# First gate of an attention and two-expert-layer kernel: no emptying of the queue at pair 12, PE pieces behind the products with the values, token rows in a queue of their own

## The chip, the cores and the metric

One Trainium2 chip, one core of it. The metric is the device time of one execution in microseconds (us). PE is TensorE, DVE is VectorE, ACT is ScalarE, POOL is GpSimd, SP is SyncE, which issues most DMAs.

## The reference

Three stages follow one another; each reads what the last one made.

```
attn  q, k, v: B=4, H=8, S=576, D=64
      s = q k^T / 8;  keep s >= max(s) - tau;  softmax over the kept;  x = attn v       -> x: 2304 tokens x 512
moe1  logits = x w_gate + log1p(exp(x w_noise)) * noise;  two best of 8 experts
      weights = softmax of these two;  out = sum of weight * (relu(x w1[e]) w2[e])       w1: 512x1024
moe2  tokens with x w_skip > 0 go to their one best expert and get weight * its output added
```

## The kernel before

*Attention.* The work is 16 pairs (a batch and two heads, laid on 128 partitions), and each pair has nine units: the 576 query rows of the two heads come as four full tiles of 128 for each head and one mixed tile. A unit makes scores S on PE (line 291), the row maximum on DVE (299), the exponential on ACT (301), the mask and sum on DVE (330), then the transposes T of the masked scores on PE (`emit_T`, 340), which ACT copies out as pt (342, 344). A pair has two chunks, and each ends in products with the values (`av`, 390 and 393, tile x) and a normalization by DVE (400, tile xT). Before that the row sums are inverted (355), POOL spreads them as rb (357, and 359 and 360 for the second chunk), and PE transposes them along with a left-over part of the scores (`extra`, 368 and 369; `extra_mixed`, 375 and 376).

A loop over the 144 units, `for u in range(NU)`, writes the instructions out in the order in which the engines take them: no scheduler moves them. In one round stand S of unit u+2, maximum and exponential of u+1, T of u-1, then products of chunks due at that time (table `AV`), then the mask of u. Counted from the start of a pair, units 2, 3, 4, 6, 7 and 8 hold products with the values; 0, 1 and 5 hold none.

*The first gate.* As soon as all tokens of some tiles are there, the gate of the first expert layer runs for them beside the next pairs: for 4 tiles after pair 3, for 5 after pair 7, for 4 after pair 11 (`GATES`); the last 5 tiles follow after attention. `gate1` is a generator: PE pieces (logits lg, their transpose, the ranks rk at lines 135 and 136), some 45 small DVE steps, and then scatters on POOL that write a token's number and weight to its expert's list in DRAM (`scatter`: a memset at 168, a DMA at 169; two for each tile). Between two scatters it waits `apart` steps. `rows1` (409) transposes a tile of tokens into rows and stores them. A generator yields 2 when its next thing is a PE piece, and 1 when this step is to end; `step(q, 1, False)` doesn't run a generator that stands before a PE piece. The gate and its rows lie in the queue `bg`, which is stepped three times in a round, the third time with PE pieces allowed.

All of these pieces, T's output and the pieces that follow write to one PSUM bank through `bank(...)`, so that each must be emptied before the next may write.

*Early experts.* At pair 12 the memory of the tokens of batches 0 and 1 is given back (`early_pool`), and the first two experts e0a and e1a prepare in it: `place_early` counts their tokens (ct, line 630; cntE, 632, then 711, 713, 715 on DVE), `load_early` loads their lists (meta, 559), `load_ids` makes the indices tid and gid (568, 570) and gathers the tokens (177), `early_xt` transposes them (xt, 584) and splits them in two (594 on ACT, 595 on DVE). `early_raw` loads weights (549, 551). After attention the weights are split (w1h, 821 on ACT; w1l, 822 on DVE or POOL) and the experts' products h (612) begin.

Of the kernel before, what the change touches and what calls it, by code (L numbers as in the profile page):

```python
# [39 lines left out]
def attention_moe_moe(ctx, tc, qT, kT, vm, vr, tau, wgn, noise, w1a, w2a, wsg, w1b, w2b, out):  # L40
# [143 lines left out]
    asked = {}  # L184

    lag = [4]
    apart = [4]

    def settle():
        for _ in range(lag[0]):  # L190
# [2 lines left out]
    def step(q, n=1, pe=True):  # L193

        while q and n > 0 and (pe or asked.get(id(q[0])) != 2):
            try:
                r = asked[id(q[0])] = next(q[0])
                n = 0 if r else n - 1
            except StopIteration:
                asked.pop(id(q.pop(0)), None)  # L200


    def pool(stack, name, bufs, side="left", **kw):
        return stack.enter_context(tc.tile_pool(name=name, bufs=bufs, side=side, reuse_waits="tile", **kw))
# [21 lines left out]
    def bank(nm):  # L226
        return banks[0](nm)
# [5 lines left out]
    def xcols(t):  # L233
        return lambda kd: xTs[t * 128 // HN][:, kd, t * 128 % HN:t * 128 % HN + 128]
# [171 lines left out]
    def rows1(t):  # L406
        ps = bank("tr")
        for kd in range(KD):
            nc.tensor.transpose(ps[:, kd * 128:(kd + 1) * 128], xcols(t)(kd), ident)
        xr = xr_p.tile([128, DM], F32, name="xr")  # L410
        nc.scalar.activation(xr, ps, AF.Copy)
        nc.sync.dma_start(x1[t * 128:(t + 1) * 128, :], xr)
# [119 lines left out]
    def expert(n, w1, w2, row0, kind, share=None):  # L532
        x = Ex()
        x.n, x.w1, x.w2, x.row0, x.kind, x.share = n, w1, w2, row0, kind, share
        x.raw, x.s1, x.s2 = (share.raw, share.s1, share.s2) if share else ({}, {}, {})
        x.native = n == 1
        x.places = share.places if share else {}
        x.ahead = x.fine = x.keep = False
        x.load = None
        x.rows = N  # L540
        x.home = None
        x.hid, x.sums, x.hh = {}, {}, None
        return x
# [9 lines left out]
    e0a, e1a = (expert(EARLY1[e], w1a, w2a, e * 128, 1) for e in range(2))  # L553
    e0a.rows, e1a.rows = 9 * 128, 13 * 128

    def load_meta(x, slots, row, small, idx=None, bufs=2):
        x.meta = small.tile([128, CAP1, 2], F32, name="meta", bufs=bufs)[:, :x.n]
        if idx is None:
            nc.sync.dma_start(x.meta, slots[row:row + x.n * 128, :].rearrange("(i p) c -> p i c", p=128))
        for i in range(0 if idx is None else x.n):  # L560
            gather(x.meta[:, i], slots, idx[:, i:i + 1])
        x.gid = small.tile([128, CAP1], I32, name="gid", bufs=bufs)[:, :x.n]
        x.tid = small.tile([128, CAP1], I32, name="tid", bufs=bufs)[:, :x.n]
# [3 lines left out]
    def load_ids(x, apart=[]):  # L567
        nc.vector.tensor_copy(x.tid, x.meta[:, :, 0])
        if x.kind == 1:
            nc.vector.tensor_scalar(x.gid, x.meta[:, :, 0], float(x.rows - 1), None, op0=OP.min)  # L570
            for i in range(x.n):
                gather(x.xs[:, i], x1, x.gid[:, i:i + 1], x.rows)
            return
        nc.gpsimd.memset(spacer, 0.0)
        for i in range(x.n):
            g = gather(x.xs[:, i], x2, x.tid[:, i:i + 1], bounds_check=N - 1, oob_is_err=False)
            for p in puts + apart:
                tc.declare_no_dep(g.ins, p.ins, reason="rows of other tokens")
            gets.append(g)

    def xt(x, i):
        ps = bank("xt")
        for kd in range(KD):
            nc.tensor.transpose(ps[:, kd * 128:(kd + 1) * 128], x.xs[:, i, kd * 128:(kd + 1) * 128], ident)
        ps = ps.rearrange("p (k c) -> p k c", k=KD)
        if x.native:
            x.xf = xp[0].tile([128, KD, 128], F32, name="xf")
            nc.scalar.activation(x.xf, ps, AF.Copy)
            return
        if i == 0:  # L590
            p, w = (x.home, x.n * 128) if x.home else (xp[0], SL1)
            x.xh, x.xl = rows2 if x.kind == 2 else (p.tile([128, KD, w], F32R, name=nm) for nm in ("xh", "xl"))
        o = x.xh[:, :, i * 128:(i + 1) * 128]
        nc.scalar.activation(o, ps, AF.Copy)  # L594
        nc.vector.tensor_tensor(x.xl[:, :, i * 128:(i + 1) * 128], ps, o.bitcast(F32), op=OP.subtract)  # L595
# [41 lines left out]
    bg = []  # L637
    fq = [fills()]
    pq, bq = [], []
# [6 lines left out]
    def at(u, phase, f, *a):  # L646
        plan.setdefault((u, phase), []).append((f, a))
# [7 lines left out]
            bg.append(f())  # L655
        return put

    WAITS = ((7, 10), (6, 0))
    GATES = {(3, 1): (0, 4), (7, 1): (4, 5), (11, 1): (9, 4)}

    def gate_and_rows(t0, n):
        rows = list(range(t0, t0 + n))
        for k, tok in enumerate(gate1(t0, n)):
            yield tok
            if k > 6 and k % 3 == 0 and rows:
                yield 2
                rows1(rows.pop(0))
                yield 1

    ectx = ExitStack()  # L670
    early = {}

    def early_pool():
        while bg:
            step(bg)
        xctx.close()
        p = early["p"] = pool(ectx, "early", 1)
        for x in (e0a, e1a):
            x.home = p
        early["h"] = [p.tile([128, AHEAD, EARLY1[0] * 128], F32R, name=nm) for nm in ("hhE", "hlE")]  # L680
# [6 lines left out]
    def load_early(x, e):  # L687
        x.xs = early["p"].tile([128, max(EARLY1), DM], F32, name="xs")
        load_meta(x, slots1, e * N, early["p"])

    def early_rows(x, e):
        yield from place_early(e)
        load_early(x, e)
        for _ in range(WAITS[e][0]):
            yield 1
        load_ids(x)
        for _ in range(WAITS[e][1]):
            yield 1

    def early_xt():  # L700
        for i in range(e0a.n):
            yield 2
            xt(e0a, i)
            yield 1

    def place_early(e):

        yield 2
        c = counts(run1, f"E{e}")
        yield  # L710
        nc.vector.tensor_scalar(c, c, -1.0, float(EARLY1[e] * 128), op0=OP.mult, op1=OP.add)
        yield
        nc.vector.tensor_scalar(c, c, 0.0, first_lane, op0=OP.max, op1=OP.mult)
        yield
        nc.vector.tensor_add(run1[:, e:e + 1], run1[:, e:e + 1], c[:, e:e + 1])
        yield
# [23 lines left out]
    for u in range(NU):  # L740
        g, c, t, hh = UNITS[u]
        if (c, t, hh) == (0, 0, 0):
            if g + 1 < len(PAIRS):
                load_v(g + 1)
            if g == 12:
                early_pool()
                fq.append(early_raw())
                bq.extend((early_rows(e0a, 0), early_xt()))
            if g == len(PAIRS) - 1:
                pq.append(early_split())  # L750
        if (c, t, hh) == (0, 0, 0) and g + 2 < len(PAIRS):
            load_qk(g + 2)
        if (c, t, hh) == (1, 3, 0) and g + 2 < len(PAIRS):
            pq.append(prep(g + 2))
        if u + 2 < NU:
            emit_S(u + 2)
        else:
            early_mm1(u + 2 - NU)
        if u + 1 < NU:
            emit_max(u + 1)  # L760
        step(bg, 1, False)
        run(u, "mid")
        if u % 2 == 0:
            emit_th(u)
        step(bg, 1, False)
        step(bq)
        if u:
            emit_T(u - 1)
        run(u, "pe")
        run(u, "end")  # L770
        emit_stt(u)
        step(pq)
        step(bg)
        if u % 4 == 3:
            step(fq)
        if (t, hh) == ((1, 1) if c == 0 else (4, 0)):
            k = (g, c)
            sums1(*k)
            at(u + 1, "mid", sums2, *k)
            at(u + 2, "pe", extra, *k)  # L780
            if c:
                at(u + 2, "pe", extra_mixed, g)
            for kt, (d, ph) in enumerate(AV[c]):
                at(u + d, ph, av, *k, kt)
            at(u + NORM[c][0], NORM[c][1], norm, *k)
            if k in GATES:
                at(u + 7, "end", bg.append, gate_and_rows(*GATES[k]))
                if k[0] == 11:
                    at(u + 7, "end", bg.append, early_rows(e1a, 1))
        if (c, t, hh) == (1, 2, 1):  # L790
            while pq:
                step(pq)
# [308 lines left out]
    for f in range(AHEAD, KF):  # L1101
# [4 lines left out]
          rows=[])  # L1106
# [340 lines left out]
    for k, x in enumerate(seq):  # L1447
        nx = seq[k + 1] if k + 1 < len(seq) else None
        rows = [r for r in seq[k + 1:k + 2] if k and not r.native] + [r for r in seq[k + 2:k + 3] if r.native]
# [56 lines left out]
```

## Time and profile before

| | |
|---|---|
| median of 3 runs | 1064.68 us (1064.45 to 1065.57) |
| the profiled execution | 1069.96 us, its span 1068.2 us |
| mean granted clock of PE | 0.977 of full speed |
| busy in the span | PE 994.7 us (93%), DVE 583.4, ACT 494.5, POOL 306.0 |
| first-gate scatters and rows | beside pairs 4 to 15 of attention |

Rows of the trace say when an instruction started (us from the span's start), how long it took, engine, line, operation, out<-in, and in brackets the engine's idle time before it and what ended it. Sixteen DMA engines serve the core; a matmul's end is modelled, so idle times of PE are good to about a tenth of a us.

### The profile page before, as it was taken

The numbers are of one execution on the slowest core, as the hardware profiler recorded it, in microseconds if no ns is written. First come the engines' busy times: TensorE is split into PE (matmuls) and PEld (weight loads), VectorE is DVE, ScalarE is ACT, GpSimd is POOL, SyncE is SP. The second block draws the span as 40 slices with busy tenths as digits, with TensorE's granted clock in tenths as the row PEclk, the third lists the DMA queues.
The fourth block names the chain that finished last, engine by engine and source line by source line (L and its number), as shares of the span: only waits on it lengthen the run. The fifth ranks groups of instructions, "written<-read, shape, count | busy, mean of one in ns | idle before, by whom it ended". The sixth has DMA issues, their size and how long they took to land. (4 is left out here: it accounts for less than half of the span.)

```text
span 1068.2 us, 16937 instructions
## 1 busy us (share of the span) xinstructions
PE 994.7 (93%) x6262; PEld 781.5 (73%) x6262; DVE 583.4 (55%) x1480; ACT 494.5 (46%) x941; POOL 306.0 (29%) x417
## 2 busy tenths in 40 slices
PE   6999999997989898999999999999999986899995
PEld 3555555554545796889889898989887775798894
DVE  6887888796776561553323342433323365577453
ACT  4766766664656441443333333333333232555352
POOL 3121143126204543221312222221322456222210
PEclk9999999998999899999999999999999998799998
DMA  6334354235320563453534445252453730766550
GB/s 151 102 87 128 109 163 88 71 93 128 122 67 1 182 194 79 130 177 90 148 77 138 111 128 120 77 158 68 109 168 78 267 115 18 283 207 197 183 220 16
DMA packets 54856, 134.76 MB, mean 126 GB/s; under 512 B 20043, under 2 KB 26475, under 8 KB 46064
## 3 DMA queue, kind: packets, MB, share of 16 engines
q1 hardware_dynamic: 41344, 107.17, 31.9%
q0 software_dynamic: 13424, 26.45, 10.8%
q8 instruction: 51, 0.84, 0.3%
q14 instruction: 37, 0.30, 0.1%
HBM read 112.64 MB, written 23.69 MB: 128 GB/s over the span
## 5 line engine op out<-in xcount | busy, mean ns | idle before, releaser
L626 DVE SCALAR_TENSOR_TENSOR hl<-h,hh 128x128 fp32r<-128x128 f32 (+3 forms) x157 | 80.1, 510 | 177.8 <-ACT hh L625 160.8
L853 PE MATMUL y<-w2h,hh 128*128 128x512 f32 x418 | 170.5, 408 | 1.2 <-ACT w2h L821 1.2
L625 ACT ACTIVATE hh<-h 128x128 fp32r<-128x128 f32 (+3 forms) x157 | 71.4, 455 | 202.2 <-PE h L612 153.3
L853 PE MATMUL y<-w2h,hl 128*128 128x512 f32 x418 | 164.3, 393 | 0.0
L853 PE MATMUL y<-w2l,hh 128*128 128x512 f32 x418 | 163.5, 391 | 0.2 <-DVE w2l L822 0.2
L612 PE MATMUL h<-xh,w1h 128*128 128x320 f32 (+2 forms) x596 | 154.7, 312 | 3.3 <-ACT xh L594 1.4
L612 PE MATMUL h<-xh,w1l 128*128 128x320 f32 (+2 forms) x596 | 152.3, 308 | 3.2 <-POOL w1l L822 3.2
L612 PE MATMUL h<-xl,w1h 128*128 128x320 f32 (+2 forms) x596 | 153.0, 309 | 1.6 <-DVE xl L595 1.6
L299 DVE TENSOR_REDUCE nm<-s 128x1 f32<-128x576 f32 x144 | 108.7, 755 | 49.9 <-PE s L291 48.9
L291 PE MATMUL s<-kr,qr 64*128 64x288 f32 (+1 forms) x640 | 112.9, 461 | 8.3 <-DVE kr L274 5.4
L301 ACT ACTIVATE e<-s,nm 128x576 f32<-128x576 f32 x144 | 106.3, 738 | 15.8 <-DVE nm L299 14.0
L342 ACT ACTIVATE pt<-tp 128x512 f32<-128x512 f32 x128 | 76.5, 597 | 74.1 <-PE tp L340 65.6
L612 PEld LDWEIGHTS h<-xh,w1h 128*128 128x128 f32 x596 | 105.9, 192 | 5.5 <-ACT xh L594 1.9
L612 PEld LDWEIGHTS h<-xh,w1l 128*128 128x128 f32 x596 | 106.1, 192 | 3.4 <-POOL w1l L822 3.4
L612 PEld LDWEIGHTS h<-xl,w1h 128*128 128x128 f32 x596 | 106.2, 192 | 2.8 <-DVE xl L595 2.7
L330 DVE SCALAR_TENSOR_TENSOR P<-s,th,e 128x576 f32<-128x576 f32 x128 | 103.4, 808 | 4.4 <-DVE foa L109 0.3
L862 POOL DMA_INDIRECT out_dram<-yo,tid x35 | 55.6, 1588 | 169.7 <-ACT yo L861 92.7
L340 PEld LDWEIGHTS tp<-ident,P 128*128 128x128 f32 x512 | 54.5, 142 | 57.1 <-issue 14.3
L853 PEld LDWEIGHTS y<-w2h,hl 128*128 128x128 f32 x418 | 78.7, 188 | 17.6
L853 PEld LDWEIGHTS y<-w2h,hh 128*128 128x128 f32 x418 | 79.0, 189 | 16.2 <-ACT w2h L821 1.7
L340 PE MATMUL tp<-ident,P 128*128 128x128 f32 x512 | 85.2, 290 | 5.1 <-DVE xl L595 2.9
L853 PEld LDWEIGHTS y<-w2l,hh 128*128 128x128 f32 x418 | 79.1, 189 | 14.5 <-DVE w2l L822 0.5
(270 smaller groups left out, 1457.4 us busy)
## 6 DMA issues: line engine op xcount, KB each, us to landing
rw<-in_w1a_dram SPq DMA_DIRECT2D x18, 1024.0 KB
rw<-in_w2a_dram SPq DMA_DIRECT2D x18, 1024.0 KB
qr<-in_qT_dram SPq DMA_DIRECT2D x30, 288.0 KB
rw<-in_w1b_dram SPq DMA_DIRECT2D x8, 1024.0 KB
rw<-in_w2b_dram SPq DMA_DIRECT2D x8, 1024.0 KB
kr<-in_kT_dram SPq DMA_DIRECT2D x96, 72.0 KB
out_dram<-zx SPq DMA_DIRECT2D x9, 512.0 KB
x<-xr SPq DMA_DIRECT2D x18, 256.0 KB
```

The costliest lines, as they stand in the source:

```text
L291: nc.tensor.matmul(s[o, i, 0:SH], qr[r, h, t * 128:min((t + 1) * 128, S)], kr[r, h if t < 4 else 2 * h], start=True, stop=True)
L299: nc.vector.tensor_reduce(nm, s, axis=AX.XY, op=OP.max, negate=True)
L301: nc.scalar.activation(e, s, AF.Exp, bias=nm)
L330: nc.vector.scalar_tensor_tensor(o.rearrange("p (a b) -> p a b", a=2), s, th, e, op0=OP.is_ge, op1=OP.mult, accum_out=a)
L340: nc.tensor.transpose(ps[:, kt], P[:, c0 + kt * 128:c0 + (kt + 1) * 128], ident)
L342: nc.scalar.activation(ch["pt"][:, :, hh, (t % 2) * 128:(t % 2 + 1) * 128], ps, AF.Copy)
L612: nc.tensor.matmul(ps[:, c, 0:m], w[:, kd, :], v[:, kd, a:a + m], start=(kd == 0 and j == 0), stop=(kd == KD - 1 and j == 2))
L625: nc.scalar.activation(dh, src, AF.Relu)
L626: nc.vector.scalar_tensor_tensor(dl, src, 0.0, dh.bitcast(F32), op0=OP.max, op1=OP.subtract)
L853: nc.tensor.matmul(y, h[:, i * 128:(i + 1) * 128], w, start=(f == 0 and j == 0), stop=(f == KF - 1 and j == 2))
L862: nc.gpsimd.indirect_dma_start(out=x2[:, :], out_offset=bass.IndirectOffsetOnAxis(ap=tid, axis=0), in_=yo, in_offset=None, compute_op=OP.a ...
```

## The change

`apart` is 2 instead of 4. Where the memory is given back at pair 12, only the rows that still wait are written out, and the gate's generator stays in its queue; the early experts' first steps (`early_rows`) go into the same queue, behind the gate. The rows of the three gates go to a queue `rq`. PE pieces are taken by `spare_pe`, which runs after the products in units 2, 3, 4, 6, 7 and 8 only: first the gate if it stands before a PE piece, else one tile of rows, else the other queues. The queue `bq` may no longer start a PE piece ahead of T. `early_ids` is split off from `early_rows` and, for the first expert, put into `bq`; `early_xt` waits until tid is there and 8 steps more. For the second expert, `early_rows` comes behind the gate of pair 11 as before.

```diff
-    apart = [4]
+    apart = [2]
...
-    WAITS = ((7, 10), (6, 0))
+    WAITS = (4, 6)
...
-    def gate_and_rows(t0, n):
+    rq = []
+
+    def gate_and_rows(t0, n, beside=False):
         rows = list(range(t0, t0 + n))
+        if beside:
+            rq.extend(rows)
+            yield from gate1(t0, n)
+            while rq:
+                yield 2
+                if rq:
+                    rows1(rq.pop(0))
+            return
...
+    def spare_pe():
+
+        if bg and asked.get(id(bg[0])) == 2:
+            step(bg)
+        elif rq:
+            rows1(rq.pop(0))
+        else:
+            step(bq)
+            step(bg)
...
     def early_pool():
-        while bg:
-            step(bg)
+        while rq:
+            rows1(rq.pop(0))
...
     def early_rows(x, e):
+        while not early:
+            yield 1
         yield from place_early(e)
+        if e == 0:
+            bq.insert(0, early_ids(x, e))
+        else:
+            yield from early_ids(x, e)
+
+    def early_ids(x, e):
         load_early(x, e)
-        for _ in range(WAITS[e][0]):
+        for _ in range(WAITS[e]):
             yield 1
         load_ids(x)
-        for _ in range(WAITS[e][1]):
-            yield 1
 
     def early_xt():
+        while not hasattr(e0a, "tid"):
+            yield 1
+        for _ in range(8):
+            yield 1
...
-                bq.extend((early_rows(e0a, 0), early_xt()))
+                bq.append(early_xt())
...
-        step(bq)
+        step(bq, 1, False)
         if u:
             emit_T(u - 1)
         run(u, "pe")
         run(u, "end")
         emit_stt(u)
         step(pq)
-        step(bg)
+        if u % 9 in (2, 3, 4, 6, 7, 8):
+            spare_pe()
+        else:
+            step(bg, 1, False)
...
-                at(u + 7, "end", bg.append, gate_and_rows(*GATES[k]))
-                if k[0] == 11:
-                    at(u + 7, "end", bg.append, early_rows(e1a, 1))
+                at(u + 7, "end", bg.append, gate_and_rows(*GATES[k], True))
+                if k[0] > 3:
+                    at(u + 7, "end", bg.append, early_rows(*((e0a, 0) if k[0] == 7 else (e1a, 1))))
```

The order of POOL at the start of pair 12, before: the last of the scatters of batch 1's gate (slots is the experts' list), and behind them the copies of the row sums, rb.

```order
L168 MEMSET spacer 1x1
L169 DMA slots_60<-mt_2864,ii_2887 18432x2
L168 MEMSET spacer 1x1
L169 DMA slots_60<-mt_2878,ii_2917 18432x2
L357 COPY rb<-sm 128x256
L359 COPY rb<-sm 128x128
L360 COPY Pm<-Pm 128x64
L357 COPY rb<-sm 128x256
L274 TENSOR_SCALAR kr<-kr,qsc 128x288 x3
```

And POOL at the same copies in the changed kernel:

```order
L274 TENSOR_SCALAR kr<-kr,qsc 128x288
L168 MEMSET spacer 1x1
L169 DMA slots_60<-mt_2878,ii_2917 18432x2
L357 COPY rb<-sm 128x256
L359 COPY rb<-sm 128x128
L360 COPY Pm<-Pm 128x64
L168 MEMSET spacer 1x1
L169 DMA slots_60<-mt_2864,ii_2887 18432x2
L168 MEMSET spacer 1x1
L169 DMA slots_60<-mt_2878,ii_2917 18432x2
```

The copies rb of pair 11's second chunk stood behind a block of eight scatters; now one scatter stands right ahead of them, behind a scaling of kr, and six scatters follow them ahead of the next rb.

The order of PE in pairs 13 and 14, with the two xt pieces of the first expert (584), as the difference of the two kernels:

```order
 L390 MATMUL x<-pt,v 64x320 x4
+L584 MATMUL xt<-ident,xs 128x128 x4
 L291 MATMUL s<-kr,qr 128x288 x2
 L340 MATMUL tp<-ident,P 128x128 x4
 L390 MATMUL x<-pt,v 64x320 x4
+L584 MATMUL xt<-ident,xs 128x128 x4
 L291 MATMUL s<-kr,qr 128x288 x2
 L340 MATMUL tp<-ident,P 128x128 x4
 L393 MATMUL x<-rr,vz_174 128x320
 L291 MATMUL s<-kr,qr 128x288 x2
-L584 MATMUL xt<-ident,xs 128x128 x4
 L340 MATMUL tp<-ident,P 128x128 x4
```

An xt piece stood between S and T and now stands between products with the values and S. The piece of the counts, ct, moves in the same way in pair 12, from between S and T of its second round to behind products of its seventh.

The order of PE at the end of attention, with the counts for the second expert, as the difference:

```order
 L375 MATMUL em<-ident,Pm 128x128
 L376 MATMUL em<-ident,rb 128x128
-L390 MATMUL x<-pt,v 64x320 x8
+L390 MATMUL x<-pt,v 64x320 x4
+L630 MATMUL ct<-run_113,ones 128x8
+L390 MATMUL x<-pt,v 64x320 x4
 L393 MATMUL x<-rr,vz_174 128x320
-L630 MATMUL ct<-run_113,ones 128x8
 L157 MATMUL lg<-xT_172,wgn_t 32x128 x16
```

The counts move from behind the last products to between them.

## Rows read from the trace of the kernel before

**Rows 1.** The page, busy time and share of the span by engine.

```profile
PE 994.7 (93%) x6262; PEld 781.5 (73%) x6262; DVE 583.4 (55%) x1480; ACT 494.5 (46%) x941; POOL 306.0 (29%) x417
```

**Rows 2.** Windows by pair: length, busy us by engine (instructions), PEclk, DMA share, GB/s.

```profile
81.44:100.04 18.60, 18.26 (x123) 9.95 (x123) 15.28 (x37) 12.75 (x22) 4.16 (x7) 1.00 0.43 127
100.04:122.35 22.31, 21.56 (x168) 12.09 (x168) 16.59 (x49) 14.53 (x28) 4.15 (x7) 1.00 0.28 89
122.35:142.33 19.98, 19.38 (x130) 10.70 (x130) 17.66 (x61) 13.88 (x25) 4.17 (x7) 1.00 0.65 198
179.75:203.47 23.72, 22.18 (x173) 12.67 (x173) 15.95 (x40) 14.86 (x29) 4.16 (x7) 1.00 0.21 61
203.47:225.29 21.82, 20.78 (x140) 11.60 (x141) 17.98 (x58) 14.56 (x26) 4.16 (x7) 1.00 0.45 122
244.33:270.48 26.15, 20.59 (x124) 11.15 (x123) 15.96 (x45) 12.80 (x22) 13.62 (x25) 0.87 0.51 135
...
292.79:317.33 24.54, 20.97 (x140) 11.64 (x142) 18.95 (x64) 15.06 (x27) 1.21 (x4) 1.00 0.24 76
```

**Rows 3.** Timeline, first half of pair 12: start, us, engine, line [idle before <-releaser].

```profile
245.61 1.02 POOL L169 DMA_INDIRECT slots<-mt,ii  x1 [0.17 <-issue]
...
246.88 0.58 SPq L549 DMA_DIRECT2D rw<-in_w1a_dram  x1
...
247.06 0.18 DVE L355 RECIPROCAL sm<-sm 128x5 f32<-128x5 f32 x1
...
249.32 0.39 PE L630 MATMUL ct<-run,ones 128*128 128x8 f32 x2
...
251.59 0.17 DVE L632 COPY cntE<-ct 128x8 f32<-128x8 f32 x1 [2.32 <-remote]
...
251.81 0.66 PE L340 MATMUL tp<-ident,P 128*128 128x128 f32 x4 [2.10 <-DVE cntE L632]
...
254.41 0.60 ACT L342 ACTIVATE pt<-tp 128x512 f32<-128x512 f32 x1 [4.51 <-remote]
254.58 0.97 POOL L169 DMA_INDIRECT slots<-mt,ii  x1 [0.23 <-issue]
255.54 0.41 POOL L357 COPY rb<-sm 128x256 f32<-128x256 f32 x1
...
256.01 0.47 PE L369 MATMUL ex<-ident,rb 128*128 128x128 f32 x1 [3.43 <-issue]
```

**Rows 4.** Timeline of clean pairs, POOL and PE: the copies and what reads them.

```profile
66.15 0.40 POOL L357 COPY rb<-sm 128x256 f32<-128x256 f32 x1 [7.25 <-DVE sm L355]
...
66.72 0.24 POOL L360 COPY Pm<-Pm 128x64 f32<-128x64 f32 x1
74.15 0.40 POOL L357 COPY rb<-sm 128x256 f32<-128x256 f32 x1 [7.19 <-DVE sm L355]
...
68.64 0.27 PE L369 MATMUL ex<-ident,rb 128*128 128x128 f32 x1
...
77.95 0.27 PE L369 MATMUL ex<-ident,rb 128*128 128x128 f32 x1
```

**Rows 5.** Timeline around the first xt piece.

```profile
307.65 0.76 PE L291 MATMUL s<-kr,qr 64*128 64x288 f32 x4
...
308.33 0.65 PE L584 MATMUL xt<-ident,xs 128*128 128x128 f32 x4
...
310.40 0.66 PE L340 MATMUL tp<-ident,P 128*128 128x128 f32 x4 [1.41 <-DVE xl L595]
```

**Rows 6.** Timeline of the end of attention and the first expert products.

```profile
350.23 0.37 SPq L559 DMA_DIRECT2D meta<-slots  x1
...
350.87 0.49 DVE L400 TENSOR_TENSOR xT<-x,rr 128x320 f32<-128x320 f32 x1 [6.24 <-PE x L393]
...
352.30 0.17 DVE L568 CAST tid<-meta 128x3 int32<-128x3 f32 x1
...
352.81 1.42 POOL L177 DMA_INDIRECT xs<-x,gid  x1 [4.72 <-PE lg L162]
...
358.11 0.58 PE L612 MATMUL h<-xh,w1l 128*128 128x256 f32 x1 [3.23 <-POOL w1l L822]
```

More of the change, by code (lines that the diff above doesn't have):

```diff
@@ L691, in early_rows, with early_xt @@
     def early_rows(x, e):
+        while not early:
+            yield 1
         yield from place_early(e)
+        if e == 0:
[3 more added lines that the diff above has]
+    def early_ids(x, e):
         load_early(x, e)
-        for _ in range(WAITS[e][0]):
+        for _ in range(WAITS[e]):
             yield 1
         load_ids(x)
-        for _ in range(WAITS[e][1]):
+    def early_xt():
+        while not hasattr(e0a, "tid"):
             yield 1
-    def early_xt():
+        for _ in range(8):
+            yield 1
         for i in range(e0a.n):
```

## The prediction, written before the changed kernel ran

> **What bounds the kernel now.** I read the page first: PE is busy for 93% of the span [rows 1], so a saving has to be a stretch in which PE idles or runs slowly. The change touches only the attention stage and its last few microseconds, so the second view is the windows, cut by pair (from the start of one pair's first row maximum, line 299, to the next pair's). In a pair with nothing extra, PE works 18.26 of 18.60 us; 0.34 us of idle is the floor. The pairs in which first-gate work is laid between the attention pieces are longer by that work's own PE time, and by more idle than the floor [rows 2]:
>
> - the pairs from 100.04 and 122.35 (numbers 5 and 6, the gate of batch 0): idle 0.75 and 0.60, so 0.41 and 0.26 above the floor;
> - from 179.75 and 203.47 (9 and 10, batch 1): 1.54 and 1.04, so 1.20 and 0.70 above;
> - from 244.33 (12, in which the queue is emptied): idle 5.56, and the only pair of these whose clock is not 1.00 but 0.87; its 26.15 us are 7.55 over a clean pair;
> - from 292.79 (14, the two early xt pieces and the gate of batch 2): idle 3.57, so 3.23 above.
>
> The third view is the timeline of pair 12 [rows 3]. Eight scatters stand on POOL one behind the other, from 245.61 to 255.55, one each (254.58-245.61)/7 = 1.28 us. The copies rb come behind them, at 255.54, though the reciprocal that they read was issued at 247.06. PE needs rb for the "ex" transposes and waits 3.43 us, until 256.01. Before that PE waits 2.10 us at the transposes of unit 1, because they share one PSUM bank with the counts and DVE took the counts out only at 251.59. In a clean pair rb starts at 66.15 and lies ready at 66.55, 2.09 us before PE wants it at 68.64; in the other chunk it is ready at 74.55, 3.40 us ahead [rows 4].
>
> **The change part by part.**
>
> *The flush (pair 12).* Before, the whole queue of batch 1's gate (its last steps and the eight scatters of rows 3) was issued at one point, and the counts and their three DVE steps came right behind. Now only waiting rows are issued there. In the new order rb stands ahead of six of the scatters, and the counts stand in unit 6 behind products with the values, which use another bank. That removes both PE waits: 2.10+3.43 = 5.53 of the 5.56 us in which PE idles there. The clock goes with them: PE had stood still for most of 250 to 256 us, and behind that the transpose of rb takes 0.47 us at 256.01 where it takes 0.27 in a clean pair, so part of the pair ran at 1.2 GHz, the lower level [rows 3, 4]. What stays is the counts' own 0.39 us. Pair 12 becomes 18.60+0.39 = 18.99: 26.15-18.99 = **-7.16**. Bounds: -3.43 (only rb's wait goes) and -7.55 (the counts hidden too). What is late next in such a pair is the ordinary work of PE. The scatters that used to hide in one block now lie between rb copies: six of them, 6x1.28 = 7.7 us, and two rb's of consecutive chunks start 74.15-66.15 = 8.0 us apart, of which the copies themselves take 66.96-66.15 = 0.81. So rb could come late by 7.7-7.2 = 0.5 us, inside its 3.40 us of slack: no cost.
>
> A rule of the Trainium skill speaks against that: in "SBUF — State Buffer", section "Who interferes with whom", a DMA issued by GpSimd has to wait while VectorE holds the ports that the two share, and one that takes about 620 ns alone took about 3100 ns. By it, as an estimate, six scatters would take 6x3.1 = 18.6 us, and the time would be that of rival 4 or more. The trace does not show it: with DVE at work beside them the scatters of pair 12 take 0.97 to 1.02 us each [rows 3].
>
> *The gate's PE pieces, behind products.* A gate piece writes the bank that emit_T uses. Where it stands between S and T, the next transposes wait until ACT has emptied that bank; where it stands behind products with the values, the next S covers the time. The gate of batch 0 has 7 pieces (logits, their transpose, four rows, ranks), which stood in units with products but for one or two and still do: 0. That of batch 1 has 10 (five tiles, so two rounds of logits); three of them stood in units 0, 1 and 5 of a pair, which have no products, and now none does. The first costs 0.41+0.26 = 0.67 us of idle above the floor, the second 1.20+0.70 = 1.90. If each costs what the first gate's do, 10x0.67/7 = 0.96: **-0.94**. Bounds: -1.90, and +0.67 (pieces closer together wait once more as the first gate's do).
>
> *Pair 14, the two xt pieces.* Each stands between S and T now, and T waits for ACT's copy and DVE's subtraction out of the shared bank: 310.40-308.33 = 2.07 us from the first piece to T, 0.65 us of it the piece itself and 1.41 a wait released by DVE; the second piece is like it [rows 5]. After the change, xt stands behind products, and S (0.76 us) lies between it and T. If the copy and the subtraction take as long, T waits 2.07-0.65-0.76 = 0.66 us for each. The gate pieces of that pair still cost what pair 6's did, 0.26. So 3.23 becomes 2x0.66+0.26 = 1.58: **-1.65**. Bounds: 0 (DVE reaches the subtraction later by the 0.76 that S covers) and -3.23 (no wait left).
>
> *The tail.* Behind the last products DVE does xT (350.87 to 351.36), six small steps (the gate's and the three of the counts for expert 1), and then tid at 352.30; gid follows, and POOL's gather starts at 352.81. POOL's split of the first weights stands behind the three gathers, and PE waits for it 3.23 us at 358.11 [rows 6]. Now the counts stand between the products, four matmuls earlier than the last ones, and the DVE steps stand ahead of xT: 352.30-351.36 = 0.94 us of DVE work leave the path to the gathers, **-0.94**. It is nothing if the metadata arrive late, whose load was issued at 350.23, behind the scatters. In the new order the last three scatters stand ahead of rb, so it is not later. Bounds: +0.5 and -3.23 (the whole wait).
>
> *Added work.* The rows' queue, the early_ids generator and the wait for tid emit the same instructions; in counts of matmuls, copies and DMAs nothing is added. On SP the weight load rw1 comes ahead of the expert's metadata, and rw2 ahead of one pair of row stores: nothing on PE waits for these within a pair. 0, and at most the 0.37 us of one issue such as the metadata's [rows 6].
>
> **Sum.** -7.16-0.94-1.65-0.94 = -10.69. The profiled execution took 1069.96 us (span 1068.2, 1.76 around it): changed, it would take 1059.3. The median of the runs shown, 1064.68, lies 5.28 below the profiled one; taking the same difference off it gives 1064.68-10.69 = **1054.0**.
>
> **The rivals.**
>
> 1. *Only the flush pays.* Pairs 9, 10 and 14 and the tail turn out to be bound by DVE steps, or the gathers of the next stage take their gain back. For it: in pair 14 the wait ends with DVE, at xl [rows 5], and DVE's order stays full. Against it: S between xt and T is 0.76 us of work that PE has to do anyway. Time: 1064.68-7.16 = 1057.5.
> 2. *The wait in pair 12 is not the flush's.* The counts had been ready since 249.71, yet DVE took them at 251.59, and ACT's copy pt started at 254.41 though its transposes had ended at 252.47: 1.88 and 1.94 us with no releaser on the core, while a 1 MB weight load from 246.88 was under way [rows 3]. If both come back wherever the stream then stands, at the same load, the gain is smaller by 1.88+1.94 = 3.8 us: 1057.8. Against it: these are the only two such waits of the stage, and the second weight load has none behind it.
> 3. *More than forecast.* In the tail POOL's split is done in time and the whole 3.23 us go, and xt waits for nothing: 1054.0-(3.23-0.94)-1.32 = 1050.4. For it: POOL is free for most of the microseconds before its gathers. Against it: the three gathers themselves stay ahead of the split.
> 4. *Slower: POOL falls behind.* The scatters now come every second step where they came every fourth, so in all three gates rb may come late as it did in pair 12. The late rb and what followed it cost 7.55-2.10 = 5.45 us there; in three gates, on top of the forecast, 1054.0+3x5.45 = 1070.4. It decides from the point where six scatters overrun the room and the slack: (8.0-0.81+3.40)/6 = 1.77 us each. At 1.28 they would have to take a third longer.
>
> 5. *It does not do what it says.* The pieces move, and their waits move with them, since what ends them is DVE, busy 15 to 19 us in each of these pairs [rows 2]. Then only the wait for rb goes: 1064.68-3.43 = 1061.3. Against it: in the clean pair DVE is just as busy, and PE idles 0.34.
>
> **How the numbers follow.** Forecast 54%, rival 1 15%, rival 2 13%, rival 3 10%, rival 4 5%, rival 5 3%. The forecast's own range is 1052 to 1056.5. To leave out no more than 2 in 10 the range has to take in rivals 1 to 3: 1049.5 to 1059.5. No change means within 0.2%, 2.1 us, about what a measurement of this kernel can tell from none. Faster by more: the forecast, rivals 1 to 3 and 1 of rival 5's 3, 93%; within 0.2%: the other 2 and 1 of rival 4's 5 (one gate late, not three), 3%; slower: the other 4%.
>
> **What would show it.** Pair 12 at 18.9 to 19.5 us with a clock of 1.00, no wait of PE at "ex" for rb, and rb at most 2.1 us (3.4 in the other chunk) behind its place in a clean pair; the counts behind products, with no wait of the next transposes. Pairs 9 and 10 with idle of 1.3 to 1.7 in all. Transposes behind xt with waits of 0.6 to 0.7 instead of 1.41 and 1.52. In the tail tid and gid right behind xT, and PE's wait for the first w1l at about 2.3 us. The forecast is wrong if rb copies come late in pairs 5, 9 or 13, if scatters take over 1.7 us each, if waits without a releaser of about 1.9 us return, or if what is won by the end of attention is lost again by the first tiles of the experts.

## The result, and the profile after

The changed kernel takes 1055.37 us (1053.55 to 1057.91, 5 runs) where the kernel before takes 1065.57 (1064.45 to 1067.59, 5 runs); the ratio is 0.9905, with a 95% interval of 0.9886 to 0.9924: 10.2 us faster, forecast 10.7. Run again beside other kernels it was 0.9912 (0.9896 to 0.9929). The profiled execution took 1054.65 us with a span of 1052.9.

The windows by pair of the changed kernel, with the columns and the pairs of [rows 2] (5, 6, 9, 10, 12, 13, 14):

```profile
99.58:122.59 23.01, 22.16 (x172) 12.45 (x171) 17.13 (x53) 15.09 (x29) 4.16 (x7) 1.00 0.30 98
122.59:141.87 19.28, 18.94 (x127) 10.59 (x128) 17.10 (x58) 13.53 (x25) 4.16 (x7) 1.00 0.66 194
179.06:201.88 22.82, 22.07 (x173) 12.59 (x173) 16.04 (x42) 14.39 (x29) 4.16 (x7) 1.00 0.19 52
201.88:223.35 21.47, 20.77 (x138) 11.54 (x138) 18.06 (x64) 15.03 (x26) 4.17 (x7) 1.00 0.48 136
242.38:263.62 21.24, 19.57 (x135) 10.74 (x133) 15.88 (x46) 13.03 (x23) 13.56 (x24) 1.00 0.64 174
263.62:284.76 21.14, 20.34 (x160) 11.29 (x156) 16.19 (x47) 14.26 (x28) 6.16 (x9) 1.00 0.44 136
284.76:309.43 24.67, 21.69 (x142) 11.91 (x144) 19.10 (x68) 15.70 (x28) 1.22 (x4) 1.00 0.21 76
```

Pairs 5 and 6 together are as long as before (42.29 us each time). Pairs 9 and 10 are 1.25 us shorter, pair 12 is 4.91 shorter and its clock is 1.00 instead of 0.87. Pair 14 is no shorter at all. The bounds of a window lie where DVE stands, while PE can be a few pieces ahead, so neighbours are read together: pairs 12 to 14 took 73.00 us and take 67.05. Pair 13 before, in the same columns:

```profile
270.48:292.79 22.31, 21.56 (x168) 12.08 (x168) 16.77 (x51) 14.54 (x28) 6.16 (x9) 1.00 0.43 137
```

The timeline of pair 12 of the changed kernel, with the columns of [rows 3]:

```profile
245.09 0.18 DVE L355 RECIPROCAL sm<-sm 128x5 f32<-128x5 f32 x1
245.93 0.41 POOL L357 COPY rb<-sm 128x256 f32<-128x256 f32 x1
...
247.92 0.27 PE L369 MATMUL ex<-ident,rb 128*128 128x128 f32 x1
...
254.12 0.76 DVE L299 TENSOR_REDUCE nm<-s 128x1 f32<-128x576 f32 x1 [2.54 <-PE tp L340]
...
255.56 0.60 ACT L342 ACTIVATE pt<-tp 128x512 f32<-128x512 f32 x1 [3.83 <-PE s L291]
...
256.21 0.66 PE L340 MATMUL tp<-ident,P 128*128 128x128 f32 x4 [1.33 <-ACT pt L342]
...
261.29 0.39 PE L630 MATMUL ct<-run,ones 128*128 128x8 f32 x2
...
262.30 0.66 PE L340 MATMUL tp<-ident,P 128*128 128x128 f32 x4
```

rb starts 0.84 us after its reciprocal was issued, where it took 8.5 [rows 3], and PE no longer waits for it. The counts stand behind products and the next transposes don't wait. A new wait stands in the middle: DVE starts a row maximum at 254.12, 1.74 us after the scores were there, ACT a copy at 255.56, 2.59 us after its transposes; T waits 1.33 us for it.

The timeline around the two xt pieces, and then of the end of attention, to be held against [rows 5] and [rows 6]:

```profile
295.08 0.66 PE L584 MATMUL xt<-ident,xs 128*128 128x128 f32 x4
...
297.15 0.66 PE L340 MATMUL tp<-ident,P 128*128 128x128 f32 x4 [0.73 <-DVE xl L595]
...
301.30 0.66 PE L340 MATMUL tp<-ident,P 128*128 128x128 f32 x4 [0.73 <-DVE xl L595]
...
303.21 0.76 PE L291 MATMUL s<-kr,qr 64*128 64x288 f32 x4 [0.72 <-DVE P L330]
...
342.50 0.49 DVE L400 TENSOR_TENSOR xT<-x,rr 128x320 f32<-128x320 f32 x1 [1.20 <-PE x L393]
...
342.90 0.16 DVE L568 CAST tid<-meta 128x3 int32<-128x3 f32 x1
...
348.47 0.55 PE L612 MATMUL h<-xh,w1l 128*128 128x256 f32 x1 [2.14 <-POOL w1l L855]
```

Behind xt the transposes wait 0.73 us instead of 1.41, but now S waits for a mask of DVE as well. In the tail tid stands right behind xT, and PE's wait for the first w1l fell from 3.23 to 2.14 us.

### The profile page after: what moved, and what is told of

The parts are those of the page before. It is cut to its first block, busy times and chain, and to the rows that moved or that the text cites. A ratio compares the mean times of both kernels' runs of the same rounds, so it can differ in the third digit from the quotient of the medians.

```text
span 1052.9 us, 16933 instructions
## 1 busy us (share of the span) xinstructions
PE 986.8 (94%) x6262; PEld 776.4 (74%) x6262; DVE 586.3 (56%) x1480; ACT 495.0 (47%) x941; POOL 305.9 (29%) x417
```

## The experiments

Each kernel ran beside the kernel before on the same chip; what counts is the ratio to it (in us: the difference of the medians).

| run | ratio, 95% interval | us against before |
|---|---|---|
| the changed kernel | 0.9905 (0.9886 to 0.9924) | -10.2 |
| e9, the same again | 0.9912 (0.9896 to 0.9929) | -8.6 |
| e3, emptying put back | 0.9972 (0.9952 to 0.9992) | -3.2 |
| e5, no emptying, new pace, old places | 0.9918 (0.9898 to 0.9937) | -8.1 |
| e8, old pace | 1.0001 (0.9986 to 1.0017) | +1.3 |
| e7, one step | 0.9936 (0.9915 to 0.9957) | -5.7 |
| e6, pieces in any unit | 0.9932 (0.9909 to 0.9954) | -6.8 |
| e1, loads later | 0.9887 (0.9864 to 0.9909) | -11.5 |
| e10, the same again | 0.9922 (0.9902 to 0.9942) | -8.0 |
| e11, and xt apart | 0.9928 (0.9907 to 0.9949) | -8.2 |
| e12, one load early | 0.9916 (0.9897 to 0.9936) | -8.7 |
| e2, before, loads later | 1.0002 (0.9986 to 1.0018) | +0.2 |

### Is it the emptying?

**e3, the changed kernel with the emptying put back.**

```diff
     def early_pool():
-        while rq:
-            rows1(rq.pop(0))
+        while len(bg) > 1:
+            step(bg)
```

> The changed kernel with the emptying put back: at pair 12 the gate's generator in the queue is run to its end before the memory is given back. Theory of the emptied queue: the remaining scatters (six or seven) stand in one block ahead of rb, PE waits for it by 3 us or more, the clock falls in that pair, pair 12 grows from 21.2 to 24 to 26 us and the time to 1059 to 1061. Theory of the loads: pair 12 stays at about 21 us and the time at 1055 to 1056.

The wait for rb and the windows of pairs 12 to 14 in e3:

```profile
254.16 0.48 PE L369 MATMUL ex<-ident,rb 128*128 128x128 f32 x1 [5.96 <-POOL rb L357]
```
```profile
242.44:269.17 26.73, 20.76 (x124) 11.17 (x123) 15.84 (x47) 12.84 (x22) 12.77 (x24) 0.87 0.50 131
269.17:295.80 26.63, 25.13 (x191) 14.09 (x191) 17.75 (x55) 16.99 (x32) 7.12 (x10) 1.00 0.50 157
295.80:318.52 22.72, 19.77 (x115) 11.11 (x116) 17.79 (x60) 12.99 (x24) 1.22 (x4) 0.85 0.08 32
```

The wait for rb is back, longer than before the change, and so is the clock of 0.87. Pair 12 is 5.5 us longer than in the changed kernel, and this is what the run shows of the emptying itself. In time 7 of the 10 us are gone, but not by pair 12 alone: the xt pieces stand in other units here (at 293.81 and 297.97), PE waits four times for 0.73 to 1.14 us between 295 and 302, the clock of pair 14 falls to 0.85, and pairs 13 and 14 together are 3.5 us longer too. Part of these 9 us is won back behind attention, so the 7 us are not the price of the emptying alone.

**e4, the kernel before with the emptying alone taken out.**

```diff
-        while bg:
-            step(bg)
...
+        while not hasattr(e0a, "tid"):
+            yield 1
...
-                bq.extend((early_rows(e0a, 0), early_xt()))
+                bg.append(early_rows(e0a, 0))
+                bq.append(early_xt())
```

> The kernel before with only the emptying taken out: the gate stays in its queue at pair 12, the first expert's rows come behind it in the same queue, its xt pieces wait for the indices; scatters keep four steps between them, PE pieces keep their old rule. Theory of the emptied queue: of the change's 10.2 us this brings pair 12's part, 5 to 7, so 1058.5 to 1060.5; the rest (gate pieces behind products, xt pieces, the tail) is missing. If the pacing or the places of the PE pieces matter as much, it brings under 3 us: over 1062.5.

In this kernel the first xt piece ran (at 279.91) before the gathers (from 284.46), so the first expert worked on rows that had not been loaded. It took 1.0124 times the kernel before; as a different computation, it says nothing on the question.

**e5, the emptying taken out and the pace doubled, the old places kept.** Unlike in e4, `early_rows` stays in `bq` and waits for the end of batch 1's gate.

```diff
-    apart = [4]
+    apart = [2]
...
-    WAITS = ((7, 10), (6, 0))
+    WAITS = ((4, 6), (6, 0))
+    done = []
...
+        done.append(t0)
...
-        while bg:
-            step(bg)
...
-        while bg:
-            step(bg)
...
     def early_rows(x, e):
+        while e == 0 and 4 not in done:
+            yield 1
```

> The kernel before with the emptying taken out and two steps between scatters instead of four; the first expert's rows wait until batch 1's gate is through, WAITS[0] is (4, 6). All gate pieces and xt pieces keep the places of before (the counts come ahead of T in unit 5 of pair 12, xt ahead of T). If places are worth what the prediction says (0.94 and 1.65 us), this brings the change's gain without them: 10.2-2.6 = 7.6 us below the kernel before. If places are worth nothing, 10 us; if they carry most, under 5.

Windows of pairs 9, 10, 12, 13 and 14 of e5, and the first wait behind xt:

```profile
179.33:203.04 23.71, 22.17 (x173) 12.65 (x174) 15.96 (x39) 14.86 (x29) 4.16 (x7) 1.00 0.22 62
203.04:224.64 21.60, 20.57 (x139) 11.54 (x138) 17.68 (x58) 14.54 (x25) 4.18 (x7) 1.00 0.46 122
243.70:262.71 19.01, 18.41 (x125) 10.01 (x124) 16.51 (x43) 12.95 (x22) 13.66 (x25) 1.00 0.91 185
262.71:285.02 22.31, 21.56 (x168) 12.09 (x167) 17.11 (x52) 14.46 (x28) 6.21 (x9) 1.00 0.49 137
285.02:309.59 24.57, 21.11 (x141) 11.78 (x142) 18.63 (x63) 15.19 (x27) 1.21 (x4) 1.00 0.24 76
```
```profile
298.40 0.66 PE L340 MATMUL tp<-ident,P 128*128 128x128 f32 x4 [1.41 <-DVE xl L595]
```

Pair 12 takes 19.01 us; the forecast had 18.99. The wait of 1.41 behind xt stays, and yet pairs 12 to 14 together take 65.89, less than in the changed kernel (67.05). These two parts, the emptying and the pace, carry most of the gain; what the places add can't be told from nothing by the times. The tail gained without them too: with the new pace the counts for the second expert come early in e5 as well, tid stands right behind xT (341.88), and PE's wait for the first w1l is that of the changed kernel:

```profile
335.79 0.17 DVE L632 COPY cntE<-ct 128x8 f32<-128x8 f32 x1
...
342.29 0.16 DVE L568 CAST tid<-meta 128x3 int32<-128x3 f32 x1
...
347.86 0.58 PE L612 MATMUL h<-xh,w1l 128*128 128x256 f32 x1 [2.10 <-POOL w1l L824]
```

### Is the new pace needed, and how far can it go?

**e8**: `apart = [4]` in the changed kernel. **e7**: `apart = [1]`.

> The changed kernel with four steps between scatters, as before the change. The counts go from unit 6 of pair 12 to unit 3 of pair 13, the gate of batch 2 waits behind batch 1's and its ranks go from unit 8 of pair 14 to unit 4 of pair 15. If the new pacing is needed for the emptying to go, the late gate's scatters fall behind the end of attention and the tail grows: 4 to 10 us above the changed kernel. If it isn't, within 1 us of it.

> The changed kernel with one step between scatters instead of two (rival 4, POOL falling behind, pushed further). At 1.28 us a scatter, ten in a row take 12.8 us, against 7.2 us between two rb copies and 3.4 of slack: if POOL's room decides, rb is late by up to 2.2 us in pair 12 with a wait of PE at the transposes of rb, and the time is 1 to 3 us above the changed kernel. If rb has more room than that, no wait at ex and the time within 1 us of the changed kernel.

The last scatter of e8 and its wait for w1l; below, the wait for rb in pair 12 of e7 and the window of that pair:

```profile
347.22 0.96 POOL L169 DMA_INDIRECT slots<-mt,ii  x1 [0.22 <-issue]
...
359.33 0.58 PE L612 MATMUL h<-xh,w1l 128*128 128x256 f32 x1 [12.46 <-POOL w1l L855]
```
```profile
251.45 0.47 PE L369 MATMUL ex<-ident,rb 128*128 128x128 f32 x1 [2.59 <-POOL rb L357]
...
242.95:266.91 23.96, 21.37 (x125) 11.52 (x124) 15.79 (x46) 12.77 (x22) 13.40 (x24) 0.86 0.55 147
```

With four steps pair 12 is clean (18.35 us), but the gate of batch 2 waits its turn behind batch 1's, its eight scatters fall behind the end of attention (338.29 to 348.18), and PE waits 12.46 us for w1l instead of 2.14. These 10.3 us are as much as the whole gain. With one step POOL falls behind, as rival 4 had it: PE waits for rb 2.59 us in pair 12, and 2.03 once more near the end of attention; in time, e7 can't be told apart from the changed kernel. Two steps lie between.

### What are the places worth?

**e6**: in the changed kernel, `spare_pe()` in all nine units.

> The changed kernel, but spare_pe may take a PE piece in every unit, units 0, 1 and 5 (without products) too. Nine pieces then stand directly ahead of the next S with no products in front, and two xt pieces come a pair earlier. Theory that places matter: each such piece leaves T a wait for the shared bank of 0.3 to 0.7 us, so 3 to 6 us slower than the changed kernel: 1058 to 1061, that is 4 to 7 below the kernel before. Theory that only the emptying matters: within 1 us of the changed kernel, 9 to 11 below before.

Windows of pairs 9 and 10 of e6:

```profile
180.70:207.27 26.57, 24.15 (x184) 13.85 (x184) 16.36 (x43) 15.99 (x32) 4.14 (x7) 1.00 0.25 75
207.27:226.84 19.57, 19.18 (x130) 10.64 (x132) 18.43 (x64) 13.80 (x25) 4.17 (x7) 1.00 0.44 112
```

These two pairs take 46.14 us: 1.85 more than in the changed kernel (44.29) and 0.83 more than in e5 (45.31). Attention ends at 331.5 us instead of 326.2. The medians show 1.8 to 3.4 us of it, against e9 and against the first measurement; the intervals overlap.

**e11**: loads later as in e1, and three more steps between the two xt pieces (`yield 1` four times instead of once).

> The changed kernel with the loads at pair 13 and three more steps between the two xt pieces, so that the second stands in unit 6 of pair 14 and not in unit 3. In the changed kernel units 3 and 4 of that pair take 5.37 and 4.22 us, and S waits 0.72 us for a mask of DVE behind the second. If DVE is crowded there because both pieces fall together, that wait goes and pair 14 shrinks by 0.5 to 1 us; if DVE has too much to do in the whole pair, it stays at 24.7 us.

Pair 14 of e11, and S behind its second xt piece:

```profile
285.17:310.02 24.85, 22.30 (x148) 12.08 (x146) 19.07 (x66) 15.68 (x29) 1.21 (x4) 1.00 0.44 160
```
```profile
310.28 0.76 PE L291 MATMUL s<-kr,qr 64*128 64x288 f32 x4 [0.55 <-DVE P L330]
```

Each xt still leaves its 0.73 us, S still waits for the mask behind the second one, 0.55 us instead of 0.72, and the pair is not shorter.

### What are the two waits in pair 12?

**e1 and e10**, the changed kernel with the first expert's weight loads queued one pair later (the same code twice); **e2**, the same edit in the kernel before; **e12**, one load ahead of pair 12's `load_qk`, the others at pair 13; **e9**, the changed kernel again.

```diff
-                fq.append(early_raw())
...
+            if g == 13:
+                fq.append(early_raw())
```

> The changed kernel with one edit: the four 1 MB weight loads of the first expert are queued at pair 13 instead of pair 12. In pair 12 of the changed kernel DVE starts a row maximum 1.74 us after its scores are there and ACT a copy 2.59 us after its transposes, with no releaser on the core, while two loads move. Theory 1 (the loads in flight hold something up that DVE and ACT need): both waits go, PE's wait of 1.33 us at the transposes with them, pair 12 shrinks from 21.2 to about 19.7 us and the time by 1 to 2 us, to 1053.5 to 1054.5. Theory 2 (the waits belong to the scatters that are left, or to DVE's order): pair 12 stays at 21.2 and the time at 1055.4.

> The kernel before, with the same edit of the loads. Theory of the emptied queue: rb stands behind eight scatters whatever the loads do and comes at the same point, so the 2.10 us at the transposes only turn into a longer wait for rb (3.43 becomes about 5), pair 12 stays at 25 to 26 us, the time within 1 us of 1065.6. Theory of the loads: most of pair 12's excess goes, the pair comes to 20 or 21 us and the time to about 1060.

> The changed kernel once more, to have it beside the next three on one chip: ratio to the kernel before 0.9905 as first measured (0.9886 to 0.9924). If the two waits without a releaser in pair 12 (DVE 1.74 us, ACT 2.59 us) come from where the loads stand in the program, they are there again and pair 12 is 21.2 us; if they are an accident of one execution, it is 19.8.

> The changed kernel with the four weight loads queued at pair 13, beside the changed kernel on the same chip. If the loads cost what pair 12 shows (1.4 us), 1 to 2 us faster than the changed kernel in the same comparison and pair 12 at 19.8 us; otherwise the same time.

> The changed kernel with one weight load ahead of pair 12's scores and keys and the other three at pair 13. Theory that bytes in flight do it: with 1 MB instead of 2 the DMA queues are empty before 252 us, the waits of DVE and ACT go and pair 12 is 19.8 us. Theory that any load near that point does it: a wait of 1.5 to 2.6 us stays and pair 12 is 21.

The window of pair 12, the same row maximum, and where there is one the copy, and the next load, in e1 and then in e10; then the wait for rb in e2:

```profile
242.31:262.16 19.85, 19.50 (x134) 10.86 (x134) 16.74 (x43) 13.00 (x23) 13.71 (x25) 1.00 0.44 80
...
252.50 0.76 DVE L299 TENSOR_REDUCE nm<-s 128x1 f32<-128x576 f32 x1 [0.85 <-PE s L291]
...
263.58 0.58 SPq L549 DMA_DIRECT2D rw<-in_w1a_dram  x1
```
```profile
243.27:265.05 21.78, 19.94 (x134) 10.85 (x134) 15.79 (x43) 12.94 (x23) 13.67 (x25) 1.00 0.39 73
...
256.58 0.76 DVE L299 TENSOR_REDUCE nm<-s 128x1 f32<-128x576 f32 x1 [3.98 <-PE s L291]
256.64 0.60 ACT L342 ACTIVATE pt<-tp 128x512 f32<-128x512 f32 x1 [3.89 <-PE s L291]
...
266.45 0.58 SPq L549 DMA_DIRECT2D rw<-in_w1a_dram  x1
```
```profile
256.39 0.47 PE L369 MATMUL ex<-ident,rb 128*128 128x128 f32 x1 [5.34 <-POOL rb L357]
```

After e1 the loads looked like the cause: the waits were gone and pair 12 took 19.85 us. e10 is the same code, no load of weights was on its way before 266.45, and both waits were there (pair 12: 21.78 us); they were there in e9, e11 and e12 too. So the loads are not the cause. That the waits went away in e1 belongs to that execution, or to its chip (e9 to e12 ran on another than e1), and not to its code. What holds DVE and ACT up is open: the waits come at the same place of the program in five of the six profiles of kernels with this order, on both engines at once, and e5 and e8, with a slightly different order, don't have them although two weight loads are on their way there too (queued at 246.32 and 245.16). Nor do the transfers tell the profiles apart that the trace lists under the kind "instruction": the one of queue q8 in this stretch starts some 8 us into pair 12 in e1, which has no waits, and in e10, which has them, and 10 us into it in the changed kernel. In e2 moving the loads changed no time: in its trace the 2.10 us at T of [rows 3] are gone, and the wait for rb is 5.34 us instead of 3.43. That is as the theory of the emptied queue had it, since rb comes when the eight scatters are through.

## Why the prediction was right, step by step

**The sum** of -10.69 was close (-10.2, and -8.6 in e9), but its terms were less so, and that it came so close is in part luck: pairs 12 to 14 gave 5.95 us of a forecast 8.81, the tail and pairs 9 and 10 more than forecast. What the two traces locate is 5.95 us in pairs 12 to 14, 1.25 in pairs 9 and 10 and 1.7 in the tail, 8.9 in all; the rest is smaller than the interval of the ratio (2 us to either side). The two profiled executions differ by 15.3 us; what goes beyond these parts lies mostly behind attention, where both kernels do the same work, and was left out by going by medians.

**The flush, -7.16.** Right in mechanism: e3 brings the wait for rb and the slow clock back, and in e5 the pair comes to 19.01 us. In the changed kernel itself pair 12 gave 4.91 and is 21.24 us long, where 18.9 to 19.5 had been named as a sign of the forecast; pairs 12 to 14 gave 5.95, where -7.16-1.65 had been forecast. Rival 2 came in part: waits without a releaser returned, which the prediction had named as a sign that it is wrong, for some 1.4 to 2 us (19.85 in e1 against 21.24 to 21.84). Its reason, the weight load, is refuted for the changed kernel.

**The gate's pieces, -0.94.** Pairs 9 and 10 went from 45.54 to 44.29: -1.25. Their idle above the floor went from 1.90 to 0.77, against 0.96 forecast. The term was right: e5, with the old places, has 45.31, so 1.02 us of it are the places'.

**The xt pieces, -1.65: the step that failed.** "T waits 2.07-0.65-0.76 = 0.66 us for each" was right (0.73). What failed is the step from there to the length of the pair. Pair 14 took 24.54 us and takes 24.67. In e5, with xt where it was, pairs 12 to 14 take 65.89; with xt behind products and without the odd waits, in e1, 19.85+21.13+24.66 = 65.64: the place is worth 0.25 us, not 1.65. When T no longer waits for DVE, S does, 0.72 us at 303.21, and e11, which spreads the pieces, leaves 0.55 of it and gains nothing either. DVE is not simply full there: it is busy for 19.10 of the 24.67 us, and in pair 11 of the kernel before it is busy for 18.07 of 19.04 while PE idles 0.26. Pair 11 before, and DVE around the second xt piece of the changed kernel:

```profile
225.29:244.33 19.04, 18.78 (x125) 10.29 (x126) 18.07 (x63) 13.14 (x24) 5.33 (x10) 1.00 0.28 62
```
```profile
300.55 0.69 DVE L595 TENSOR_TENSOR xl<-xt,xh 128x512 fp32r<-128x512 f32 x1 [1.64 <-ACT xh L594]
...
302.33 0.82 DVE L330 SCALAR_TENSOR_TENSOR P<-s,th,e 128x576 f32<-128x576 f32 x1
```

DVE idles 1.64 us until ACT has made xh, then does xl in 0.69 us; the row maximum (301.32) and the mask that S waits for (302.33) stand behind xl in its order, although the scores for them were there at 300.57. The time that T no longer waits for xl comes back at S. This is read from the trace; no run took xl out of DVE's order.

**The tail, -0.94.** From the start of the last row maximum to the first product with w1l it was 358.11-334.1 = 24.0 us, and is 348.47-326.2 = 22.3: -1.7. The six DVE steps left the path, as forecast, and PE's wait is 2.14 (2.3 forecast). What the forecast missed is that the pace of the scatters decides here. In the prediction the pace was a danger for POOL; e5 and e8 show that it is what pays: with it and the old places e5's tail is 347.86-326.32 = 21.5 us, and without it e8's is 359.33-327.95 = 31.4, 9.1 more than in the changed kernel.

**Rival 4** (POOL falls behind) did not come at two steps: scatters take 0.97 to 1.02 us in pair 12 of the changed kernel, and no rb is late. e7 bears out its working: at one step PE waits 2.59 us for rb, and up to 2.2 had been expected.

No version tried here beats the changed kernel by more than the measurement can tell.

## What to carry to other kernels

A queue emptied at one point costs what stands behind it on the slowest engine that it fills: here eight scatters of 1.28 us ahead of copies that PE needs. But taking the emptying out only pays if the queue then drains as fast as work comes in; look for what waits for its last item. And a wait that is shortened on PE shortens the stage only if the work that ended it doesn't hold up PE's next piece instead: look first at what stands behind that work in the other engine's order. That engine's busy time alone does not tell.

## What was not expected of the hardware

DVE and ACT stood still together in pair 12 for 1.7 to 3.2 us after their inputs were ready (DVE at 254.12 in the changed kernel, at 256.58 in e10, with scores done at 253.41). The trace names no releaser but PE pieces that had ended by then. It was so in five of six profiles of the same instruction order, and not in the sixth, with or without a transfer of weights on its way. One profile without such a wait is no proof that an edit removed it: the same code ran at 19.85 and at 21.78 us for this pair. In pair 12 the granted clock was 1.00 where PE waited 1.33 us at T, and 0.86 and 0.87 where it waited 2.59 (e7) and 5.96 us (e3) for rb. But the longest wait does not decide alone: in pair 14 of e3 it was 0.85 behind four waits of at most 1.14 us, close together.
